# Sliding-window attention beside a gated MLP: exponentials of four steps in one buffer, far scores eight key blocks at a time

## The chip, the cores and the metric

The kernel runs on one core of a Trainium2 chip. The metric is the device time of one execution in microseconds, a median of several runs. The profile is one execution of its own, with every engine's instructions: TensorE (PE, and PEld for its weight loads), VectorE (DVE), ScalarE (ACT), GpSimd (POOL) and SyncE (SP), which only issues DMAs here.

## What is computed

The input has 2048 tokens of 512 features, in bf16. One branch is causal attention with 32 heads of 16 features and a window of 256 tokens, the other a gated MLP with 1376 hidden features. A sigmoid gate g per token mixes them.

```python
def _A_ref(x, wqkv, wo):
    H = 32; Dh = D // H; W = 256
    ...
    scores = jnp.einsum("bhqd,bhkd->bhqk", q, k) * (Dh ** -0.5)
    mask = (idx[:, None] - idx[None, :] >= 0) & (idx[:, None] - idx[None, :] < W)
    scores = jnp.where(mask[None, None], scores, -1e9)
    p = _softmax(scores, axis=-1)
    o = jnp.einsum("bhqk,bhkd->bhqd", p, v)
    return (o as B, S, D) @ wo

def _B_ref(x, w1, w3, w2):
    h = silu(x @ w1) * (x @ w3)
    return h @ w2

g = _sigmoid((x * gate_w).sum(-1, keepdims=True))
return g * a + (1 - g) * b
```

## The kernel before

**One order for all engines, made by a planner.** Nothing is issued where it stands in the source. Every piece of work is an `Op` with an engine, an assumed duration, its dependencies, a due time and the buffers it takes and frees. `Plan.emit` is a list scheduler: it steps through assumed time, and on the engine that can start first it picks, among the ops that can start within 0.02 us of that, the one with the earliest due time. The order that comes out is what each engine executes, first in, first out; the real waits are semaphores. The due times come from four constants: attention is spread from `T0` over `TA` microseconds (`at(c, t)`), the MLP from `TF0` to `TF1`.

**Attention.** The 32 heads are cut into four head groups c of eight heads (128 features), one after another, and the tokens into 16 steps t of 128. Scores are held transposed, keys in partitions and queries in columns. The keys of a step are two blocks of 64; a block of 64 keys of two heads fills 128 partitions (`kbd`, with zeros so that each head meets its own features), and four such pairs of heads run in the four 32-row groups of TensorE.

- `projections(c, tq)`: Q, K and V for a quarter of the tokens (tq = 0 to 3). K goes through VectorE (`kt`, L404) and two GpSimd multiplications (`kbd`, L407), for c = 0 through VectorE and ScalarE; Q is cast by VectorE (L418), V by ScalarE and VectorE (L437, L439).
- `main_batch(c, t)`: for both key blocks of a step, the scores against the block's own 64 queries and the 192 that follow, 8 matmuls of 256 columns (L464) into `su`, one buffer of four PSUM banks. Two exponentials on ScalarE (L469), two banks each, write columns 0 to 255 of an `E` buffer. VectorE masks the diagonal block with a minimum against `mdiag` (L476).
- `far_batch(c, g)`: the last, partly masked 64 queries of each key block (queries 256 to 319 after the block's start), for four key blocks at once: 16 matmuls of 64 columns (L499) into the same `su`, two exponentials (L504) into columns 256 to 319 of the two steps' `E` buffers, and two GpSimd affine selects for each (L512), one for each half of the partitions.
- `pv(c, i)`: for 128 queries, the products of up to six `E` slices with the values, 24 matmuls (L542) into a `ch` bank; the values carry a column of ones, so the softmax's sum comes along. VectorE takes the reciprocal (L550) and multiplies with it and with the gate (L553). SyncE transposes the result into `OT` by DMA (L559).

There are six `E` buffers, one taken by each step and freed by the pv two steps later.

**MLP and output.** For each quarter of the tokens, 11 blocks of hidden features: a gate chain (`gps`, one bank) and an up chain (`ups`, one bank) of four matmuls each (L603), a tanh on ScalarE (L608), and two VectorE products (L612 frees `gps`, L616 frees `ups`). Then w2 (L638), 11 matmuls for 128 tokens into a `ch` bank, scaled into `bsb` by VectorE (L642). The output projection (L662) needs `OT` of all four head groups; VectorE adds `bsb` (L666) and SyncE stores.

PSUM is full: `su` has four banks, `gps` and `ups` one each, and two `ch` banks serve projections, pv, w2 and output projection in turn. The score groups of all steps, main and far, go through the one `su`: a group's matmuls wait until the exponentials of the group before have read all of it.

Of the kernel before, what the change touches and what calls it, by code (L numbers as in the profile page):

```python
# [8 lines left out]
ACT = mybir.ActivationFunctionType  # L9
BF16 = mybir.dt.bfloat16  # L10
# [5 lines left out]
P = 128  # L16
KB = 64
# [20 lines left out]
class Plan:  # L38
# [73 lines left out]
def kernel(  # L112
# [12 lines left out]
    nc = tc.nc  # L125
# [13 lines left out]
    NE = 6  # L139
# [19 lines left out]
    kbd = pp.tile([P, NKB, 2, KB], BF16, name="kbd")  # L159
# [112 lines left out]
    def at(c, t):  # L272
        return T0 + step * (c * NT + t)
# [90 lines left out]
    ejob = {}  # L364

    def projections(c, tq):
# [52 lines left out]
        a = add("PE", 0.864, lambda: chain(qj, 0, 4), src + qwar, due, take=[(qj, "ch")])  # L419
        q_ready[(c, tq)] = add("DVE", 0.69, qev, [a], due, free=[(qj, "ch")])  # L420

        vj = Job()

# [24 lines left out]
            res.append(prev)  # L448
        v_ready[(c, tq)] = res

    def main_batch(c, t):
        due = at(c, t)
        job = Job()
        ej = ejob[(c, t)] = Job()
        wid = 256 if t < NT - 1 else P
        tqs = sorted({min(NTC - 1, (P * t) // 512), min(NTC - 1, (P * t + 319) // 512)})
        deps = list(k_ready[(c, t // 4)]) + [q_ready[(c, q)] for q in tqs]

        def mm():
            for par in range(2):  # L460
                q0 = KB * (2 * t + par)
                for s in range(4):
                    r = slice(32 * s, 32 * s + 32)
                    nc.tensor.matmul(su[:, s, par * wid:(par + 1) * wid],  # L464
                                     lhsT=kbd[r, 2 * t + par, :, :].rearrange("p a k -> p (a k)"),
                                     rhs=qT[r, q0:q0 + wid], start=True, stop=True)

        def ex(h):
            nc.scalar.activation(  # L469
                out=E[ej.at["E"]][:, 2 * h:2 * h + 2, :, 0:wid],  # L470
                in_=su[:, 2 * h:2 * h + 2, 0:2 * wid].rearrange("p s (a q) -> p s a q", a=2),
                func=ACT.Exp, scale=SCALE)

        def mask():
            e = E[ej.at["E"]][:, :, :, 0:KB].rearrange("p s a q -> p (s a) q")
            nc.vector.tensor_tensor(out=e, in0=e, in1=mdiag[:, None, :].to_broadcast([P, 8, KB]),  # L476
                                    op=ALU.min)
# [6 lines left out]
        return add("DVE", 0.42, mask, [x0, x1], due)  # L484

    def far_batch(c, g):
        t1 = 2 * g + 1
        due = at(c, t1) + 0.3
        job = Job()
        tq = min(NTC - 1, (P * (2 * g) + 511) // 512)  # L490
        deps = [q_ready[(c, min(NTC - 1, (KB * (4 * g + j) + 319) // 512))] for j in range(4)]
        deps += k_ready[(c, g // 2)]

        def mm():
            for j in range(4):
                q0 = KB * (4 * g + j) + 256
                for s in range(4):
                    r = slice(32 * s, 32 * s + 32)
                    nc.tensor.matmul(su[:, s, j * KB:(j + 1) * KB],  # L499
                                     lhsT=kbd[r, 4 * g + j, :, :].rearrange("p a k -> p (a k)"),  # L500
                                     rhs=qT[r, q0:q0 + KB], start=True, stop=True)

        def ex(i):
            nc.scalar.activation(  # L504
                out=E[ejob[(c, 2 * g + i)].at["E"]][:, :, :, 256:320],
                in_=su[:, :, i * P:(i + 1) * P].rearrange("p s (a q) -> p s a q", a=2),
                func=ACT.Exp, scale=SCALE)

        def mask(i):
            e = E[ejob[(c, 2 * g + i)].at["E"]][:, :, :, 256:320].rearrange("p s a q -> p (s a) q")  # L510
            for lo in (0, KB):
                nc.gpsimd.affine_select(out=e[lo:lo + KB], in_=e[lo:lo + KB], pattern=[[0, 8], [-1, KB]],  # L512
                                        compare_op=ALU.is_ge, fill=0.0, base=-1, channel_multiplier=1)

        a = add("PE", 0.4, mm, deps + [su_ops[(c, t1)]], due, take=[(job, "su")])
        far_ops[(c, g)] = a
        res = []
        for i in range(2):
            x = add("ACT", 0.54, lambda i=i: ex(i), [a], due, free=[(job, "su")])
            res.append(add("POOL", 1.28, lambda i=i: mask(i), [x], due))  # L520
        return res

    def pv(c, i, main, far):
        due = at(c, i) + 0.6
# [12 lines left out]
        def mm():  # L537
            po = ch[job.at["ch"]]
            for s in range(4):
                for bi, (t, par, off) in enumerate(blocks):  # L540
                    e = E[ejob[(c, t)].at["E"]][:, s].rearrange("p a q -> p (a q)")
                    nc.tensor.matmul(po[:, 34 * s:34 * s + 34], lhsT=e[:, off:off + P],  # L542
                                     rhs=vbd[:, 2 * t + par, s, :], start=(bi == 0),
                                     stop=(bi == len(blocks) - 1))
# [26 lines left out]
        ot_ready[(c, i)] = add("SP", 1.1, tr, [d], due, free=[(job, "oc")], lat=1.6)  # L571

    for c in range(NDC):
        main, far = {}, {}
        for tq in range(NTC):
            projections(c, tq)
        for t in range(NT):
            main[t] = main_batch(c, t)
            if t % 2 == 1 and t < NT - 2:
                far[t - 1], far[t] = far_batch(c, t // 2)  # L580
# [126 lines left out]
```

## Time and profile before

| what | value |
|---|---|
| runs before | 264.07, 263.88, 263.87 us; median 263.88 |
| the profiled execution | 264.46 us |
| its span, first to last instruction | 262.4 us |
| TensorE's granted clock | 1.000 |
| main score groups (L464) / far score groups (L499) / pv (L542) | 64 / 28 / 64 |
| main exponentials, 128 partitions x 1024 (L469) | 120, mean 1022 ns; 8 narrower ones of the last steps, 594 ns |
| far exponentials, 128 x 512 (L504) | 56, mean 595 ns |
| kbd multiplications on GpSimd, 128 x 512 (L407) | 24, mean 1605 ns |
| GpSimd affine select, 128 x 128 (ident, L191) | 1, 294 ns |
| TensorE idle before a score group, released by ScalarE (L464 and L499) | 1.4 us in all |

How to read it: the page gives for each engine its busy time as a share of the span, and then groups of instructions by line, engine and operation with count, total and mean duration, and the idle time of the engine just before them with what ended it. A matmul's end is modelled, and matmuls overlap, so durations of TensorE's groups do not add up; differences between starts do. In a list in order of time, the first number is the start in microseconds from the span's beginning and the second the length; a bracket at the end gives the engine's idle time before and what ended it. For TensorE's line numbers: L464 main scores, L499 far scores, L542 pv, L603 gate and up, L638 w2, L383 Q and K, L429 V, L662 output projection.

### The profile page before, as it was taken

How to read it: one execution, taken by the hardware profiler on the slowest of the kernel's cores; microseconds unless marked ns; L12 is line 12 of the kernel's file. 1: busy time of each engine (PE TensorE's matmuls, PEld its weight loads, DVE VectorE, ACT ScalarE, POOL GpSimd, SP SyncE). 2: the span in 40 equal slices, each digit the busy share in tenths (PEclk: the TensorE clock that was granted, in tenths of full speed). 3: DMA queues.
4: the chain of work that ended last, by engine and by line, in shares of the span. 5: the costliest groups of instructions: out<-in, count | busy, mean ns of one | idle time of the engine just before them, and what ended most of it. 6: DMA issues, size and time to landing. Idle time of an engine off the chain costs nothing.

```text
span 262.4 us, 8242 instructions
## 1 busy us (share of the span) xinstructions
PE 249.0 (95%) x3447; PEld 138.2 (53%) x3501; DVE 174.8 (67%) x393; ACT 190.3 (73%) x271; POOL 116.1 (44%) x157
## 2 busy tenths in 40 slices
PE   8999999999999999999999999999989999999992
PEld 8455564654555555555455445564546454455540
DVE  4576977845578867755487775766468867765652
ACT  3278798787677797777768888777677787776640
POOL 6003223662736635782273683751736233332220
PEclk9999999999999999999999999999999999999999
DMA  7999950000001000000000000000000111110112
GB/s 192 267 246 258 223 132 9 13 12 10 8 8 21 8 8 14 11 8 13 6 18 13 8 10 13 14 12 6 13 8 18 45 34 52 50 33 27 50 52 65
DMA packets 27933, 13.14 MB, mean 50 GB/s; under 512 B 17305, under 2 KB 27897, under 8 KB 27897
## 3 DMA queue, kind: packets, MB, share of 16 engines
q1 hardware_dynamic: 27896, 12.63, 21.6%
q8 instruction: 27, 0.44, 0.7%
q14 instruction: 10, 0.07, 0.1%
HBM read 6.85 MB, written 2.10 MB: 34 GB/s over the span
## 4 chain that ended last, share of the span: by engine, by line
PE 86%; ACT 3%; DVE 3%; DMA 2%; POOL 2%; issue 2%; SPq 0%
PE ch L638 14%; PE ch L542 14%; PE gps L603 14%; PE ups L603 13%; PE ch L383 10%; PE su L464 7%; PE ch L429 5%; PE ch L662 5%; DMA OT<-oc 2%; PE su L499 2%; ACT E L469 2%; POOL kbd L407 1%; PE su L225 1%; POOL E L512 1%; ACT vbd L437 1%
## 5 line engine op out<-in xcount | busy, mean ns | idle before, releaser
L469 ACT ACTIVATE E<-su 128x1024 bf16<-128x1024 f32 (+1 forms) x128 | 122.5, 995 | 28.0 <-PE su L464 27.6
L512 POOL TENSOR_SCALAR_AFFINE_SELECT E<-E 64x512 bf16<-64x512 bf16 x112 | 73.5, 656 | 107.3 <-ACT E L504 87.9
L542 PEld LDWEIGHTS <-E 128*128 128x128 bf16 x1440 | 43.3, 96 | 12.9 <-issue 4.6
L407 POOL TENSOR_SCALAR kbd<-kt,rowsA 128x512 bf16<-128x512 bf16 x24 | 38.3, 1605 | 26.5 <-DVE kt L404 11.9
L603 PEld LDWEIGHTS <-w_sb 128*128 128x128 bf16 (+1 forms) x352 | 31.3, 99 | 33.6 <-issue 4.8
L542 PE MATMUL ch<-vbd,E 128*128 128x34 bf16 x1440 | 46.4, 177 | 0.6 <-POOL E L512 0.4
L603 PE MATMUL gps<-xT,w_sb 128*128 128x512 bf16 (+1 forms) x163 | 43.5, 379 | 1.3 <-DVE h L612 0.5
L603 PE MATMUL ups<-xT,w_sb 128*128 128x512 bf16 (+1 forms) x156 | 43.0, 380 | 1.1 <-issue 0.2
L638 PE MATMUL ch<-w_sb,hT 128*128 128x512 bf16 (+1 forms) x161 | 42.6, 380 | 1.2 <-issue 0.5
L504 ACT ACTIVATE E<-su 128x512 bf16<-128x512 f32 x56 | 30.4, 595 | 13.4 <-PE su L499 12.1
L612 DVE SCALAR_TENSOR_TENSOR h<-tt,gps 128x512 bf16<-128x512 bf16 (+1 forms) x44 | 29.8, 678 | 14.8 <-ACT tt L608 14.1
L476 DVE TENSOR_TENSOR E<-E,mdiag 128x512 bf16<-128x512 bf16 x64 | 27.9, 437 | 16.1 <-ACT E L469 16.0
L608 ACT ACTIVATE tt<-gps 128x512 bf16<-128x512 f32 (+1 forms) x44 | 26.3, 598 | 13.5 <-PE gps L603 12.6
L616 DVE SCALAR_TENSOR_TENSOR hT<-h,ups 128x512 bf16<-128x512 bf16 (+1 forms) x44 | 29.9, 681 | 5.7 <-PE ups L603 4.4
L383 PE MATMUL ch<-xT,wqkv_sb 128*128 128x512 bf16 x126 | 32.5, 380 | 0.1
L464 PE MATMUL su<-qT,kbd 32*128 32x256 bf16 (+1 forms) x512 | 25.0, 269 | 1.6 <-ACT E L469 1.2
L550 DVE RECIPROCAL rden<-ch 128x8 f32<-128x8 f32 x64 | 13.1, 204 | 18.1 <-PE ch L542 17.8
L638 PEld LDWEIGHTS <-hT 128*128 128x128 bf16 (+1 forms) x176 | 14.9, 97 | 16.6 <-issue 2.9
L553 DVE SCALAR_TENSOR_TENSOR oc<-ch,gq,rden 128x128 bf16<-128x128 f32 x64 | 22.3, 349 | 1.5
L383 PEld LDWEIGHTS <-wqkv_sb 128*128 128x128 bf16 x128 | 11.5, 98 | 13.6 <-issue 1.4
L662 PE MATMUL ch<-wo_sb,OT 128*128 128x512 bf16 x60 | 16.1, 380 | 2.3 <-DMA OT<-oc 1.5
L464 PEld LDWEIGHTS <-kbd 32*128 32x128 bf16 x512 | 7.9, 92 | 19.3 <-issue 18.1
(55 smaller groups left out, 154.8 us busy)
## 6 DMA issues: line engine op xcount, KB each, us to landing
out_dram<-ot SPq DMA_DIRECT2D x16, 128.0 KB, 1.8
wqkv_sb<-in_A_wqkv_dram SPq DMA_DIRECT2D x6, 256.0 KB, 5.2
w_sb<-in_B_w_dram SPq DMA_DIRECT2D x1, 1280.0 KB, 7.1
w_sb<-in_B_w_dram SPq DMA_DIRECT2D x2, 608.0 KB, 5.3
w_sb<-in_B_w_dram SPq DMA_DIRECT2D x2, 512.0 KB, 6.8
OT<-oc SPq DMA_TRANSPOSE x64, 2.3
xs<-in_A_x_dram SPq DMA_DIRECT2D x2, 256.0 KB, 3.0
w_sb<-in_B_w_dram SPq DMA_DIRECT2D x2, 256.0 KB, 4.4
```

The source lines that it names most:

```text
L383: nc.tensor.matmul(pst[:], lhsT=wqkv_sb[:, dc, col + c * P:col + (c + 1) * P], rhs=xT[:, dc, tq * 512:(tq + 1) * 512], start=(dc == 0), st ...
L407: nc.gpsimd.tensor_scalar_mul(out=kv[:, :, h, :], in0=kt[kj.at["kt"]][:].rearrange("p (k t) -> p k t", t=KB), scalar1=rowsA[:, h:h + 1])
L464: nc.tensor.matmul(su[:, s, par * wid:(par + 1) * wid], lhsT=kbd[r, 2 * t + par, :, :].rearrange("p a k -> p (a k)"), rhs=qT[r, q0:q0 + wi ...
L469: nc.scalar.activation(out=E[ej.at["E"]][:, 2 * h:2 * h + 2, :, 0:wid], in_=su[:, 2 * h:2 * h + 2, 0:2 * wid].rearrange("p s (a q) -> p s ...
L504: nc.scalar.activation(out=E[ejob[(c, 2 * g + i)].at["E"]][:, :, :, 256:320], in_=su[:, :, i * P:(i + 1) * P].rearrange("p s (a q) -> p s ...
L512: nc.gpsimd.affine_select(out=e[lo:lo + KB], in_=e[lo:lo + KB], pattern=[[0, 8], [-1, KB]], compare_op=ALU.is_ge, fill=0.0, base=-1, chann ...
L542: nc.tensor.matmul(po[:, 34 * s:34 * s + 34], lhsT=e[:, off:off + P], rhs=vbd[:, 2 * t + par, s, :], start=(bi == 0), stop=(bi == len(bloc ...
L603: nc.tensor.matmul(dst[0:fs, :], lhsT=w[:, dc, f * P:f * P + fs], rhs=xT[:, dc, tcb * 512:(tcb + 1) * 512], start=(dc == 0), stop=(dc == N ...
L612: nc.vector.scalar_tensor_tensor(out=h1[job.at["h1"]][0:fs, :], in0=tt[job.at["tt"]][0:fs, :], scalar=1.0, in1=gps[0:fs, :], op0=ALU.add, ...
L616: nc.vector.scalar_tensor_tensor(out=hT[0:fs, f, :], in0=h1[job.at["h1"]][0:fs, :], scalar=0.5, in1=ups[0:fs, :], op0=ALU.mult, op1=ALU.mult)
L638: nc.tensor.matmul(bps[:], lhsT=hT[0:fs, f, mm * P:(mm + 1) * P], rhs=w2_sb[0:fs, f, :], start=(f == 0), stop=(f == NFC - 1))
L662: nc.tensor.matmul(pso[:], lhsT=OT[:, c, m * P:(m + 1) * P], rhs=wo_sb[:, c, :], start=(c == 0), stop=(c == NDC - 1))
```

## The change

`E` becomes two buffers, each for a quad of four steps (eight key blocks). A quad takes its buffer once, in an op without an instruction (`quad`, on an engine "EQ" that exists for the planner alone), and every pv frees the quads that it reads. A main step has one exponential over all four banks. The far scores of a quad's eight key blocks are one group: 32 matmuls that fill `su`, one exponential, and two affine selects over all eight blocks of the quad (the last quad of a head group has only four key blocks: 16 matmuls, half an exponential, and selects of the full size). The far batch no longer waits for a main batch of its own quad, and stands ahead of them in the list. Q of the later quarters gets an earlier due time, and the four constants of the due times change. In the order that the planner makes of it, each head group has 16 main and 4 far score groups, and a far group follows the first main group of its quad, for head group 0, quad 0 the second.

```diff
-    E = [pp.tile([P, 4, 2, 384], BF16, name=f"E_{i}") for i in range(NE)]
+    E = [pp.tile([P, 4, 8, 384], BF16, name=f"E_{i}") for i in range(2)]
...
-        for i in range(NE):
-            nc.gpsimd.memset(E[i][:, :, 0, 320:384], 0.0)
+        for e in E:
+            for s in range(4):
+                nc.gpsimd.memset(e[:, s, 0:8:2, 320:384], 0.0)
...
-    T0, TA, TF0, TF1 = 12.0, 218.0, 6.0, 252.0
+    T0, TA, TF0, TF1 = 9.0, 222.0, 6.0, 246.0
...
-            war += [far_ops.get((c - 1, g)) for g in (2 * tq, 2 * tq + 1)]
+            war.append(far_ops[(c - 1, tq)])
...
         qj = Job()
+        qdue = due if tq == 0 else at(c, 4 * tq - 4) - lead + 4.0
...
-    def main_batch(c, t):
+    def quad(c, h):
+
+        job = ejob[(c, h)] = Job()
+        return add("EQ", 0.0, lambda: None, [], at(c, 4 * h) - 1.0, take=[(job, "E")], lat=0.0)
+
+    def main_batch(c, t, room):
         due = at(c, t)
         job = Job()
-        ej = ejob[(c, t)] = Job()
+        ej = ejob[(c, t // 4)]
+        j0 = 2 * (t % 4)
...
-        def ex(h):
+        def ex():
             nc.scalar.activation(
-                out=E[ej.at["E"]][:, 2 * h:2 * h + 2, :, 0:wid],
-                in_=su[:, 2 * h:2 * h + 2, 0:2 * wid].rearrange("p s (a q) -> p s a q", a=2),
+                out=E[ej.at["E"]][:, :, j0:j0 + 2, 0:wid],
+                in_=su[:, :, 0:2 * wid].rearrange("p s (a q) -> p s a q", a=2),
                 func=ACT.Exp, scale=SCALE)
 
         def mask():
-            e = E[ej.at["E"]][:, :, :, 0:KB].rearrange("p s a q -> p (s a) q")
-            nc.vector.tensor_tensor(out=e, in0=e, in1=mdiag[:, None, :].to_broadcast([P, 8, KB]),
+            e = E[ej.at["E"]][:, :, j0:j0 + 2, 0:KB]
+            nc.vector.tensor_tensor(out=e, in0=e, in1=mdiag[:, None, None, :].to_broadcast([P, 4, 2, KB]),
                                     op=ALU.min)
...
-        x0 = add("ACT", d, lambda: ex(0), [a], due, take=[(ej, "E")], free=[(job, "su")])
-        x1 = add("ACT", d, lambda: ex(1), [a, x0], due, free=[(job, "su")])
+        x0 = add("ACT", 1.8 if wid == 256 else 1.0, ex, [a, room], due, free=[(job, "su")])
...
-    def far_batch(c, g):
-        t1 = 2 * g + 1
-        due = at(c, t1) + 0.3
+    def far_batch(c, h, room):
+
+        due = at(c, 4 * h) + 0.3
...
+        nb = min(8, NKB - 4 - 8 * h)
+        deps = [q_ready[(c, q)] for q in range(h, min(NTC, h + 2))] + k_ready[(c, h)]
 
         def mm():
-            for j in range(4):
-                q0 = KB * (4 * g + j) + 256
+            for j in range(nb):
+                q0 = KB * (8 * h + j) + 256
...
-        def ex(i):
+        def ex():
             nc.scalar.activation(
-                out=E[ejob[(c, 2 * g + i)].at["E"]][:, :, :, 256:320],
-                in_=su[:, :, i * P:(i + 1) * P].rearrange("p s (a q) -> p s a q", a=2),
+                out=E[ej.at["E"]][:, :, 0:nb, 256:320],
+                in_=su[:, :, 0:nb * KB].rearrange("p s (j q) -> p s j q", q=KB),
                 func=ACT.Exp, scale=SCALE)
 
-        def mask(i):
-            e = E[ejob[(c, 2 * g + i)].at["E"]][:, :, :, 256:320].rearrange("p s a q -> p (s a) q")
+        def mask():
+            e = E[ej.at["E"]][:, :, :, 256:320].rearrange("p s j q -> p (s j) q")
             for lo in (0, KB):
-                nc.gpsimd.affine_select(out=e[lo:lo + KB], in_=e[lo:lo + KB], pattern=[[0, 8], [-1, KB]],
+                nc.gpsimd.affine_select(out=e[lo:lo + KB], in_=e[lo:lo + KB],
+                                        pattern=[[0, 32], [-1, KB]],
                                         compare_op=ALU.is_ge, fill=0.0, base=-1, channel_multiplier=1)
 
-        a = add("PE", 0.4, mm, deps + [su_ops[(c, t1)]], due, take=[(job, "su")])
-        far_ops[(c, g)] = a
-        res = []
-        for i in range(2):
-            x = add("ACT", 0.54, lambda i=i: ex(i), [a], due, free=[(job, "su")])
-            res.append(add("POOL", 1.28, lambda i=i: mask(i), [x], due))
-        return res
+        a = add("PE", 0.52 if nb == 8 else 0.4, mm, deps, due, take=[(job, "su")])
+        far_ops[(c, h)] = a
+        x = add("ACT", 1.8 if nb == 8 else 1.0, ex, [a, room], due, free=[(job, "su")])
+        return [add("POOL", 5.2, mask, [x], due)] * (nb // 2)
...
-        frees = []
-        if i >= 2:
-            frees.append((ejob[(c, i - 2)], "E"))
-        if i == NT - 1:
-            frees += [(ejob[(c, i - 1)], "E"), (ejob[(c, i)], "E")]
+        frees = [(ejob[(c, h)], "E") for h in range(max(0, i - 2) // 4, i // 4 + 1)]
```

More of the change, by code (lines that the diff above doesn't have):

```diff
@@ L138 @@
     SCALE = float(DH) ** -0.5
-    NE = 6
     WARM = 28
@@ L182 @@
     ch = [ps.tile([P, 512], F32, name=f"ch_{i}") for i in range(2)]
-    plan = Plan({"su": 1, "g": 1, "u": 1, "ch": 2, "E": NE, "kt": 2, "tt": 2, "h1": 2,
+    plan = Plan({"su": 1, "g": 1, "u": 1, "ch": 2, "E": 2, "kt": 2, "tt": 2, "h1": 2,
                  "oc": 8, "ot": 2, "hT": 1})
@@ L371, in projections @@
             war = [su_ops[(c - 1, t)] for t in range(4 * tq, 4 * tq + 4)]
-            war += [far_ops.get((c - 1, g)) for g in (2 * tq, 2 * tq + 1)]
+            war.append(far_ops[(c - 1, tq)])
             vwar = [pv_ops[(c - 1, i)] for i in range(4 * tq, min(NT, 4 * tq + 6))]
             qwar = [su_ops[(c - 1, t)] for t in range(max(0, 4 * tq - 3), 4 * tq + 4)]
-            qwar += [far_ops.get((c - 1, g)) for g in range(max(0, 2 * tq - 2), 2 * tq + 2)]
+            qwar += [far_ops[(c - 1, h)] for h in range(max(0, tq - 1), tq + 1)]
         else:
@@ L415, in projections @@
         qj = Job()
+        qdue = due if tq == 0 else at(c, 4 * tq - 4) - lead + 4.0
         def qev():
             nc.vector.tensor_copy(out=qT[:, tq * 512:(tq + 1) * 512], in_=ch[qj.at["ch"]][:])
-        a = add("PE", 0.864, lambda: chain(qj, 0, 4), src + qwar, due, take=[(qj, "ch")])
-        q_ready[(c, tq)] = add("DVE", 0.69, qev, [a], due, free=[(qj, "ch")])
+        a = add("PE", 0.864, lambda: chain(qj, 0, 4), src + qwar, qdue, take=[(qj, "ch")])
+        q_ready[(c, tq)] = add("DVE", 0.69, qev, [a], qdue, free=[(qj, "ch")])
         vj = Job()
@@ L466, in mm @@
                                      rhs=qT[r, q0:q0 + wid], start=True, stop=True)
-        def ex(h):
+        def ex():
             nc.scalar.activation(
-                out=E[ej.at["E"]][:, 2 * h:2 * h + 2, :, 0:wid],
-                in_=su[:, 2 * h:2 * h + 2, 0:2 * wid].rearrange("p s (a q) -> p s a q", a=2),
+                out=E[ej.at["E"]][:, :, j0:j0 + 2, 0:wid],
+                in_=su[:, :, 0:2 * wid].rearrange("p s (a q) -> p s a q", a=2),
                 func=ACT.Exp, scale=SCALE)
         def mask():
-            e = E[ej.at["E"]][:, :, :, 0:KB].rearrange("p s a q -> p (s a) q")
-            nc.vector.tensor_tensor(out=e, in0=e, in1=mdiag[:, None, :].to_broadcast([P, 8, KB]),
+            e = E[ej.at["E"]][:, :, j0:j0 + 2, 0:KB]
+            nc.vector.tensor_tensor(out=e, in0=e, in1=mdiag[:, None, None, :].to_broadcast([P, 4, 2, KB]),
                                     op=ALU.min)
         a = add("PE", 0.42 if wid == 256 else 0.31, mm, deps, due, take=[(job, "su")])
-        d = 0.833e-3 * 4 * wid + 0.1
-        x0 = add("ACT", d, lambda: ex(0), [a], due, take=[(ej, "E")], free=[(job, "su")])
-        x1 = add("ACT", d, lambda: ex(1), [a, x0], due, free=[(job, "su")])
+        x0 = add("ACT", 1.8 if wid == 256 else 1.0, ex, [a, room], due, free=[(job, "su")])
         su_ops[(c, t)] = a
-        return add("DVE", 0.42, mask, [x0, x1], due)
-    def far_batch(c, g):
-        t1 = 2 * g + 1
-        due = at(c, t1) + 0.3
+        return add("DVE", 0.42, mask, [x0], due)
+    def far_batch(c, h, room):
+        due = at(c, 4 * h) + 0.3
         job = Job()
-        tq = min(NTC - 1, (P * (2 * g) + 511) // 512)
-        deps = [q_ready[(c, min(NTC - 1, (KB * (4 * g + j) + 319) // 512))] for j in range(4)]
-        deps += k_ready[(c, g // 2)]
+        ej = ejob[(c, h)]
+        nb = min(8, NKB - 4 - 8 * h)
+        deps = [q_ready[(c, q)] for q in range(h, min(NTC, h + 2))] + k_ready[(c, h)]
         def mm():
-            for j in range(4):
-                q0 = KB * (4 * g + j) + 256
+            for j in range(nb):
+                q0 = KB * (8 * h + j) + 256
                 for s in range(4):
@@ L499, in mm @@
                     nc.tensor.matmul(su[:, s, j * KB:(j + 1) * KB],
-                                     lhsT=kbd[r, 4 * g + j, :, :].rearrange("p a k -> p (a k)"),
+                                     lhsT=kbd[r, 8 * h + j, :, :].rearrange("p a k -> p (a k)"),
                                      rhs=qT[r, q0:q0 + KB], start=True, stop=True)
-        def ex(i):
+        def ex():
             nc.scalar.activation(
-                out=E[ejob[(c, 2 * g + i)].at["E"]][:, :, :, 256:320],
-                in_=su[:, :, i * P:(i + 1) * P].rearrange("p s (a q) -> p s a q", a=2),
+                out=E[ej.at["E"]][:, :, 0:nb, 256:320],
+                in_=su[:, :, 0:nb * KB].rearrange("p s (j q) -> p s j q", q=KB),
                 func=ACT.Exp, scale=SCALE)
-        def mask(i):
-            e = E[ejob[(c, 2 * g + i)].at["E"]][:, :, :, 256:320].rearrange("p s a q -> p (s a) q")
+        def mask():
+            e = E[ej.at["E"]][:, :, :, 256:320].rearrange("p s j q -> p (s j) q")
             for lo in (0, KB):
-                nc.gpsimd.affine_select(out=e[lo:lo + KB], in_=e[lo:lo + KB], pattern=[[0, 8], [-1, KB]],
+                nc.gpsimd.affine_select(out=e[lo:lo + KB], in_=e[lo:lo + KB],
+                                        pattern=[[0, 32], [-1, KB]],
                                         compare_op=ALU.is_ge, fill=0.0, base=-1, channel_multiplier=1)
-        a = add("PE", 0.4, mm, deps + [su_ops[(c, t1)]], due, take=[(job, "su")])
-        far_ops[(c, g)] = a
-        res = []
-        for i in range(2):
-            x = add("ACT", 0.54, lambda i=i: ex(i), [a], due, free=[(job, "su")])
-            res.append(add("POOL", 1.28, lambda i=i: mask(i), [x], due))
-        return res
+        a = add("PE", 0.52 if nb == 8 else 0.4, mm, deps, due, take=[(job, "su")])
+        far_ops[(c, h)] = a
+        x = add("ACT", 1.8 if nb == 8 else 1.0, ex, [a, room], due, free=[(job, "su")])
+        return [add("POOL", 5.2, mask, [x], due)] * (nb // 2)
     def pv(c, i, main, far):
@@ L540, in mm @@
                 for bi, (t, par, off) in enumerate(blocks):
-                    e = E[ejob[(c, t)].at["E"]][:, s].rearrange("p a q -> p (a q)")
+                    e = E[ejob[(c, t // 4)].at["E"]][:, s, 2 * (t % 4):2 * (t % 4) + 2, :].rearrange("p a q -> p (a q)")
                     nc.tensor.matmul(po[:, 34 * s:34 * s + 34], lhsT=e[:, off:off + P],
@@ L573 @@
     for c in range(NDC):
-        main, far = {}, {}
+        main = {}
         for tq in range(NTC):
             projections(c, tq)
[L577 to L580, printed above, removed]
+        far = []
+        for h in range(NTC):
+            room = quad(c, h)
+            far += far_batch(c, h, room)
+            for t in range(4 * h, 4 * h + 4):
+                main[t] = main_batch(c, t, room)
         for i in range(NT):
```

## The prediction

> **What bounds the kernel now.** I read the page's busy line first, then TensorE's instructions in order of time, then the waits, then VectorE and GpSimd around the masks.
>
> ```profile
> span 262.4 us, 8242 instructions
> PE 249.0 (95%) x3447; PEld 138.2 (53%) x3501; DVE 174.8 (67%) x393; ACT 190.3 (73%) x271; POOL 116.1 (44%) x157
> ...
> L469 ACT ACTIVATE E<-su 128x1024 bf16<-128x1024 f32 (+1 forms) x128 | 122.5, 995 | 28.0 <-PE su L464 27.6
> L512 POOL TENSOR_SCALAR_AFFINE_SELECT E<-E 64x512 bf16<-64x512 bf16 x112 | 73.5, 656 | 107.3 <-ACT E L504 87.9
> ...
> L476 DVE TENSOR_TENSOR E<-E,mdiag 128x512 bf16<-128x512 bf16 x64 | 27.9, 437 | 16.1 <-ACT E L469 16.0
> ```
>
> TensorE is busy in 95% of the span and every other engine has idle time. ScalarE's exponentials wait for TensorE (27.6 us before L469), not the other way. So shortening ScalarE pays only where TensorE waits for it.
>
> ```profile
> 228.30 1.03 PE L603 MATMUL gps<-xT,w_sb 128*96 128x512 bf16 x4
> 229.26 0.40 PE L464 MATMUL su<-qT,kbd 32*128 32x256 bf16 x8
> 229.59 0.77 PE L542 MATMUL ch<-vbd,E 128*128 128x34 bf16 x24
> 230.21 1.02 PE L662 MATMUL ch<-wo_sb,OT 128*128 128x512 bf16 x4
> 231.06 1.03 PE L603 MATMUL ups<-xT,w_sb 128*96 128x512 bf16 x4
> 232.02 0.30 PE L499 MATMUL su<-qT,kbd 32*128 32x64 bf16 x16
> 232.25 0.77 PE L542 MATMUL ch<-vbd,E 128*128 128x34 bf16 x24
> ```
>
> Columns: start, length, work. Read starts to starts, since lengths overlap. Four matmuls of 512 columns take 0.86 us (230.21 to 231.06), but 0.96 if a score group follows (228.30 to 229.26): 0.10 to enter a score group. A main group takes 0.33, a far group of 16 takes 0.23, a pv of 24 takes 0.62 (0.69 before a score group), a v projection 0.89.
>
> I priced the whole issue order with these steps: 250.05 us. TensorE's first matmul starts at 1.04 and its last ends near 258.55, so it waits 258.55 - 1.04 - 250.05 = 7.5 us. Comparing the starts of all 92 score groups with the priced order places them: 0.8 us before 15 us, 4.6 between 15 and 245, 2.1 at the end. After the last matmul come 3.85 us of evacuation and store. That is the check on my ruler: 250.05 + 1.04 + 0.8 + 4.6 + 2.1 + 3.85 = 262.4.
>
> **The change, part by part.**
>
> *Far scores in batches of eight.* The changed order has 16 far groups (12 of 32 matmuls, 4 of 16) for 28. A group of 32 moves as many columns as a main group of 8x256, so I take 0.34; two old groups, 0.46, are the other bound (12 x 0.12 = 1.4 us more). Far matmuls go from 28 x 0.23 = 6.44 to 12 x 0.34 + 4 x 0.23 = 5.0, and 12 entries of 0.10 vanish. The same pricing over the changed order gives 247.5 us: 2.6 off TensorE's own path.
>
> *One exponential for four banks.* One of 1024 elements takes 1.022 us, one of 512 takes 0.594: 0.836 ns an element and 0.166 fixed, so 2048 take 1.88. The old pair overlaps itself and takes 1.94 (two at 186.64 end at 188.58). The score banks are thus held 0.06 us less; the main group before a far group holds them for as long as before, and a wide far exponential holds them 1.88 for 1.08. Start to start a score group now needs 0.33 + 0.12 (to ScalarE) + 1.88 + 0.06 (back) = 2.39. Along the new order all but five gaps give that; those lack 0.48, 0.30, 0.21, 0.08 and 0.07. The 0.30 comes ahead of a wait counted below, so 0.8. Where a pv follows its own main mask too early, six places lack 1.3 together. So 2.1 new against the 4.6 of old waits in the middle, which were made by another order; some of those go. I take 5.5 for both, bounds 3.5 and 6.7.
>
> *Shared E buffers.* A quad needs the buffer of two quads earlier. Its first writer starts 2.5 us or more of TensorE work after the last pv that read it, in every quad. Nothing.
>
> *Moved Q projections, and the new due times.* They show only in the order. The clearest part is the end.
>
> ```profile
> 254.45 0.76 PE L542 MATMUL ch<-vbd,E 128*128 128x34 bf16 x24
> 255.39 0.81 PE L662 MATMUL ch<-wo_sb,OT 128*128 128x512 bf16 x2 [0.18 <-DVE ot L666]
> 256.48 1.04 PE L662 MATMUL ch<-wo_sb,OT 128*128 128x512 bf16 x4 [0.28 <-DMA OT<-oc]
> 258.34 0.39 PE L662 MATMUL ch<-wo_sb,OT 128*128 128x512 bf16 x1 [0.82 <-DMA OT<-oc]
> ```
>
> Now the last output projections wait for the transposing DMA of the last pv. In the changed order 22 w2 matmuls (4.7 us) and a projection lie between the last pv and the last two projections, longer than reciprocal, product and DMA (about 3 us). I leave 0.3 of the 2.1.
>
> *The far mask, which speaks against the change.* It is one affine select on 64x2048 for four on 64x512. From 128x128 (0.294) to 512 elements (0.657) it costs 0.945 ns an element, so 2.11 us; bounds 2.1 and 4 x 0.657 = 2.63. GpSimd's total falls (32 x 2.11 = 67.5 for 73.5), but one instruction is three times as long. What that does to VectorE:
>
> ```profile
> 169.22 0.66 POOL L512 TENSOR_SCALAR_AFFINE_SELECT E<-E 64x512 bf16<-64x512 bf16 x1
> ...
> 169.28 0.87 DVE L476 TENSOR_TENSOR E<-E,mdiag 128x512 bf16<-128x512 bf16 x1 [0.33 <-ACT E L469]
> ...
> 186.58 3.13 POOL L407 TENSOR_SCALAR kbd<-kt,rowsA 128x512 bf16<-128x512 bf16 x2 [0.90 <-DVE kt L404]
> ...
> 188.76 0.41 DVE L476 TENSOR_TENSOR E<-E,mdiag 128x512 bf16<-128x512 bf16 x1
> ```
>
> The main mask L476, usually 0.42, took 0.87 when it began 0.06 us into an affine select, and ended 0.27 after that one's end. Another, at 146.29, took 0.80 and ended 0.28 after its affine select. A third, at 154.09, began 0.15 before an end and lost nothing. So the mask stands still until the running select is over. Only three of 64 masks met one. Under kbd (L407) it does not stand still: 12 of 16 overlaps cost nothing, the worst 0.18.
>
> The Trainium skill, "SBUF — State Buffer", section "Who interferes with whom", says that a VectorE instruction with two SBUF inputs and a GpSimd instruction that reads SBUF exclude each other for the whole instruction. The select rows agree with it; the kbd rows do not. By the rule the sum is the likeliest case below, by the kbd rows the first rival.
>
> In the new order the meeting is built in. Count from the end of a far group of 32. Its exponential ends at 0.12 + 1.88 = 2.00; the two selects run 2.08 to 6.36. The next main group starts at about 2.44, its exponential runs from 2.9 to 4.8, its mask would start at 4.85, inside the second select, and ends at 6.63 in place of 5.27: 1.36 late. The pv that reads it can start at 6.70. Behind a far group of 16 (exponential 1.02) the bound is 5.88. When does TensorE reach that pv? For head group 1, quad 1: pv 0.62 + gate 0.86 + projection 0.96 + main 0.33 + up 0.86 + gate 0.86 + v 0.89 = 5.38, so it waits 1.3. All 16 in turn (0 where it comes later): 0, 0.50, 0, 0.31; 0.65, 1.32, 0.92, 0.07; 1.51, 1.35, 0.27, 1.17; 2.00, 0.92, 0.05, 1.17. Sum 12.2 us. Behind the late mask VectorE has the up and gate products, the Q and K casts and the pv quotients queued; TensorE's wait of about the same length gives them their time back, except where the wait is short, and there they may add some. Bounds of this part: 3.1 if a mask never loses more than the 0.45 seen (the pv can then start at 5.80, or 4.94 behind a far group of 16), and 16 x 1.36 = 21.8 if VectorE's whole delay reaches TensorE. I take 12.2, by the three rows that end with the select.
>
> In this case a pv that waits lets the others' producers catch up, so of the 5.5 I keep 3.5.
>
> *Sum*, against the profiled span: 247.5 + 1.04 + 0.8 + 3.5 + 12.2 + 0.3 + 3.85 = 269.2, that is 6.8 more than 262.4. The profiled run took 264.46 in all, the median of the runs is 263.88; on that, 270.7 us. The two other edits, mask constants at the start and the wider mask operand on VectorE (again 512 elements), cost nothing: the constants run while TensorE waits for loads, and 0.1 us more on a mask would be 0.1 per short pv, 1.2 at most.
>
> **Rivals.**
>
> *The mask slips past long selects* (as under kbd). Then the 12.2 is gone and 5.5 stays: 259.0 span, 260.5 us, faster. For it: GpSimd has room and 12 of 16 kbd overlaps are free. Against it: every mask that met a select early in it stood still. It decides for gain once the mean loss at a pv falls below 0.2 us.
>
> *The mask loses at most 0.45.* Then 3.1 + 5.5: 262.1 span, 263.6 us, level with before. For it: no longer loss has been seen; against it: none could be, with selects of 0.66.
>
> *VectorE's delay spreads.* If each 1.36 reaches TensorE also through the gate bank (freed by L612) and the two ch banks, 21.8 for 12.2: 280.3 us. For it: gate and up have one bank each. Against it: VectorE is 67% busy and catches up.
>
> **How the numbers follow.** Likeliest case 0.62, slips past 0.23, at most 0.45 lost 0.12, spreads 0.03. Its own range is 267 to 274 (3.5 to 6.7 of other waits, far groups at 0.46). The range for 8 in 10 has to reach into the first rival: 260.0 to 274.0. A measurement here tells about 0.2%, 0.5 us, from no change. Faster: 0.23 of the first rival and half of the second's 0.12, less a little for the bound: 0.29. Same 0.06. Slower: 0.62 and 0.03: 0.65.
>
> **What would show it.** Right: affine selects near 2.1 us; some 14 to 16 main masks of 1 to 2.2 us, each ending 0.27 after a select; TensorE idle before pv with VectorE's mask or GpSimd as releaser, about 10 to 14 us; no wait on the DMA in the last projections; 80 score groups, a far group of 32 starting its successor 0.34 later. Wrong: masks all near 0.42, or selects well under 1.6 us (the second would end before the mask), and then a time near 260.5.

## The result, and the profile after

The changed kernel takes 276.16 us (275.92 to 276.2) against 263.88: a ratio of 1.0462, interval 1.0444 to 1.0481. It is slower, as forecast, but by 12.3 us instead of 6.8, and the time lies 2.2 us above the range.

The page of the changed kernel, its span, busy times and three groups:

```profile
span 274.1 us, 8026 instructions
...
PE 248.6 (91%) x3450; PEld 137.3 (50%) x3501; DVE 198.2 (72%) x393; ACT 183.0 (67%) x167; POOL 110.4 (40%) x79
...
L517 POOL TENSOR_SCALAR_AFFINE_SELECT E<-E 64x2048 bf16<-64x2048 bf16 x32 | 67.8, 2120 | 119.1 <-ACT E L509 118.1
L483 DVE TENSOR_TENSOR E<-E,mdiag 128x512 bf16<-128x512 bf16 x64 | 48.4, 756 | 16.7 <-ACT E L476 16.7
L545 PE MATMUL ch<-vbd,E 128*128 128x34 bf16 x1440 | 48.1, 178 | 11.6 <-DVE E L483 8.4
```

ScalarE and GpSimd became less busy, VectorE 23 us busier, although it has the same 393 instructions. Most of that is in one line: the 64 main masks, 27.9 us before, take 48.4 us. At 0.415 us for an undisturbed one, 21.8 us of it is standing still.

The waits of TensorE after (engine, line, what it waited for; us in all, times, longest), from 0.5 us on, without the start and its own issue:

```profile
PE ch L545 <- DVE E L483: 8.4, 9, 1.5
PE gps L604 <- DVE h L613: 2.0, 3, 1.1
...
PE ch L383 <- DVE vbd L440: 1.0, 1, 1.0
PE ch L639 <- DVE vbd L440: 1.0, 1, 1.0
PE ch L545 <- DVE bsb L643: 1.0, 2, 0.8
...
PE ch L545 <- DVE vbd L440: 0.8, 1, 0.8
...
PE ch L545 <- DVE kt L404: 0.7, 1, 0.7
...
PE ch L545 <- DVE ot L667: 0.5, 1, 0.5
```

The first line is the forecast mechanism, pv waiting for the mask it reads. The others shown add up to 7.0 us, and none of them names the mask: a gate bank or a `ch` bank was not emptied in time by VectorE. Some 2 us of the 7.0 do not come from the change of the selects; e2 below has them too.

One of the stuck masks, in head group 3 (start, length, work, idle time before; instructions of several engines):

```profile
205.63 4.28 POOL L517 TENSOR_SCALAR_AFFINE_SELECT E<-E 64x2048 bf16<-64x2048 bf16 x2 [9.90 <-ACT E L509]
206.06 1.88 ACT L476 ACTIVATE E<-su 128x2048 bf16<-128x2048 f32 x1 [0.50 <-PE su L471]
...
207.97 2.21 DVE L483 TENSOR_TENSOR E<-E,mdiag 128x512 bf16<-128x512 bf16 x1 [0.19 <-ACT E L476]
...
210.24 0.52 PE L545 MATMUL ch<-vbd,E 128*128 128x34 bf16 x14 [1.45 <-DVE E L483]
```

The second select ends at 205.63 + 4.28 = 209.91, the mask at 210.18: 0.27 later. In 15 of 16 quads there is such a mask, and all 15 end 0.26 to 0.28 after a select. They stand still for 20.4 us together, 1.36 on the mean; most of the rest of the 21.8 is three other masks that met a kbd multiplication (last section).

### The profile page after: what moved, and what is told of

The parts are those of the page before. It is cut to its first block, busy times and chain, and to the rows that moved or that the text cites. A ratio compares the mean times of both kernels' runs of the same rounds, so it can differ in the third digit from the quotient of the medians.

```text
span 274.1 us, 8026 instructions
## 1 busy us (share of the span) xinstructions
PE 248.6 (91%) x3450; PEld 137.3 (50%) x3501; DVE 198.2 (72%) x393; ACT 183.0 (67%) x167; POOL 110.4 (40%) x79
## 4 chain that ended last, share of the span: by engine, by line
PE 69%; DVE 15%; ACT 9%; issue 5%; another core or an unknown queue 0%; ACTq 0%
PE ch L545 13%; PE ups L604 11%; PE gps L604 10%; PE ch L639 10%; PE ch L383 8%; DVE E L483 7%; ACT E L476 6%; PE su L471 6%; PE ch L663 5%; PE ch L430 3%; DVE vbd L440 2%; PE su L504 2%; DVE bsb L643 1%; ACT vbd L438 1%; PE su L225 1%
## 5 line engine op out<-in xcount | busy, mean ns | idle before, releaser
L476 ACT ACTIVATE E<-su 128x2048 bf16<-128x2048 f32 x64 | 116.6, 1822 | 44.3 <-PE su L471 44.0
L517 POOL TENSOR_SCALAR_AFFINE_SELECT E<-E 64x2048 bf16<-64x2048 bf16 x32 | 67.8, 2120 | 119.1 <-ACT E L509 118.1
L483 DVE TENSOR_TENSOR E<-E,mdiag 128x512 bf16<-128x512 bf16 x64 | 48.4, 756 | 16.7 <-ACT E L476 16.7
L545 PE MATMUL ch<-vbd,E 128*128 128x34 bf16 x1440 | 48.1, 178 | 11.6 <-DVE E L483 8.4
L407 POOL TENSOR_SCALAR kbd<-kt,rowsA 128x512 bf16<-128x512 bf16 x24 | 37.6, 1579 | 26.4 <-DVE kt L404 23.2
L639 PE MATMUL ch<-w_sb,hT 128*128 128x512 bf16 (+1 forms) x165 | 42.0, 379 | 2.1 <-DVE vbd L440 1.0
L613 DVE SCALAR_TENSOR_TENSOR h<-tt,gps 128x512 bf16<-128x512 bf16 (+1 forms) x44 | 30.0, 681 | 10.8 <-ACT tt L609 10.0
L383 PE MATMUL ch<-xT,wqkv_sb 128*128 128x512 bf16 x122 | 31.9, 379 | 1.5 <-DVE vbd L440 1.0
L509 ACT ACTIVATE E<-su 128x2048 bf16<-128x2048 f32 (+1 forms) x16 | 26.6, 1662 | 8.4 <-PE su L504 8.4
L553 DVE RECIPROCAL rden<-ch 128x8 f32<-128x8 f32 x64 | 13.1, 204 | 12.7 <-PE ch L545 12.2
L643 DVE TENSOR_SCALAR bsb<-ch,omg 128x512 bf16<-128x512 f32 x16 | 11.8, 747 | 8.3 <-PE ch L639 8.2
```

Source lines behind the costliest of these rows:

```text
L407: nc.gpsimd.tensor_scalar_mul(out=kv[:, :, h, :], in0=kt[kj.at["kt"]][:].rearrange("p (k t) -> p k t", t=KB), scalar1=rowsA[:, h:h + 1])
L476: nc.scalar.activation(out=E[ej.at["E"]][:, :, j0:j0 + 2, 0:wid], in_=su[:, :, 0:2 * wid].rearrange("p s (a q) -> p s a q", a=2), func=ACT ...
L483: nc.vector.tensor_tensor(out=e, in0=e, in1=mdiag[:, None, None, :].to_broadcast([P, 4, 2, KB]), op=ALU.min)
L509: nc.scalar.activation(out=E[ej.at["E"]][:, :, 0:nb, 256:320], in_=su[:, :, 0:nb * KB].rearrange("p s (j q) -> p s j q", q=KB), func=ACT.E ...
L613: nc.vector.scalar_tensor_tensor(out=h1[job.at["h1"]][0:fs, :], in0=tt[job.at["tt"]][0:fs, :], scalar=1.0, in1=gps[0:fs, :], op0=ALU.add, ...
L639: nc.tensor.matmul(bps[:], lhsT=hT[0:fs, f, mm * P:(mm + 1) * P], rhs=w2_sb[0:fs, f, :], start=(f == 0), stop=(f == NFC - 1))
```

## The experiments

Each run's middle waits are TensorE's waits from its first score group to its last, read as in the prediction: starts of the score groups against the issue order at undisturbed prices. Mask delay is the busy time of VectorE's main masks beyond 0.415 us each.

| kernel | median us | ratio to before (interval) | mask delay | middle waits |
|---|---|---|---|---|
| before | 263.88 | | 1.4 | 4.6 |
| changed | 276.16 | 1.0462 (1.0444 to 1.0481) | 21.8 | 21.1 |
| e1, selects cut in four | 261.12 | 0.9884 (0.9869 to 0.9900) | 4.0 | 6.2 |
| e2, memset for select | 260.93 | 0.9870 (0.9851 to 0.9890) | 1.6 | 5.3 |
| e3, far mask on VectorE | 265.32 | 1.0037 (1.0024 to 1.0051) | 1.9 | 9.4 |
| e4, before plus long selects | 280.73 | 1.0630 (1.061 to 1.065) | 26.8 | 19.3 |
| e5, latency told | 273.31 | 1.0346 (1.0301 to 1.0391) | 19.5 | 15.6 |
| e6, busy time told | 271.37 | 1.0286 (1.0260 to 1.0312) | 16.1 | 15.0 |
| e7, cut, old T0 and TA | 266.87 | 1.0105 (1.0060 to 1.0151) | 4.2 | 10.7 |
| e8, cut, exponential halved | 261.64 | 0.9913 (0.9894 to 0.9932) | 3.7 | 6.4 |
| e9, stuck mask on GpSimd | 261.20 | 0.9882 (0.9853 to 0.9911) | 2.4 | 5.6 |
| e10, cut, latency told | 264.08 | 1.0007 (0.9991 to 1.0022) | 3.8 | 6.1 |
| e11, cut, mask on GpSimd | 263.70 | 0.9975 (0.9961 to 0.9988) | 1.4 | 7.7 |

### e1: the far selects cut in four

```diff
-            e = E[ej.at["E"]][:, :, :, 256:320].rearrange("p s j q -> p (s j) q")
-            for lo in (0, KB):
-                nc.gpsimd.affine_select(out=e[lo:lo + KB], in_=e[lo:lo + KB],
-                                        pattern=[[0, 32], [-1, KB]],
+            for s in range(4):
+                e = E[ej.at["E"]][:, s, :, 256:320]
+                for lo in (0, KB):
+                    nc.gpsimd.affine_select(out=e[lo:lo + KB], in_=e[lo:lo + KB],
+                                            pattern=[[0, 8], [-1, KB]],
```

> The changed kernel with each far select cut into four of 64x512; order of all other work unchanged. Theory A (a main mask stands still until the running select ends, and VectorE's queue behind it hands the delay to TensorE): a mask can lose at most about 0.5 us instead of 2.1, so the 21.8 us of mask delay fall to about 5, and the time to 264 to 267 us. Theory B (the new order and due times cost the time, whatever the selects do): 276 us, unchanged.

261.12 us, 15 us less with TensorE's order unchanged, and faster than before. The page of this run:

```profile
L518 POOL TENSOR_SCALAR_AFFINE_SELECT E<-E 64x512 bf16<-64x512 bf16 x128 | 86.2, 673 | 103.7 <-ACT E L509 97.2
L483 DVE TENSOR_TENSOR E<-E,mdiag 128x512 bf16<-128x512 bf16 x64 | 30.6, 478 | 17.6 <-ACT E L476 17.5
```

GpSimd works 18 us more than in the changed kernel (86.2 for 67.8), and the kernel is 15 us faster: the length of one select decided, not their sum. Theory B (order and due times) falls. The time lies under the 264 to 267 of Theory A: masks still lose 4.0 us, 1.9 of them under the short selects and nearly all the rest under kbd multiplications, but that hardly reaches TensorE (middle waits 6.2 against 5.3 in e2).

### e2: memsets in the selects' place

```diff
-                nc.gpsimd.affine_select(out=e[lo:lo + KB], in_=e[lo:lo + KB],
-                                        pattern=[[0, 32], [-1, KB]],
-                                        compare_op=ALU.is_ge, fill=0.0, base=-1, channel_multiplier=1)
+                nc.gpsimd.memset(e[lo:lo + KB], 0.0)
```

> The changed kernel with the far selects replaced by GpSimd memsets of the same elements, which write and do not read (the far scores are left out of the sums). Order and dependencies unchanged, GpSimd busy nearly as long. Theory A: main masks back to 0.42 us each, TensorE's waits in the middle down from 21 to about 5 us, 260 to 262 us. Theory B: 276 us. If GpSimd being late with the far mask were the cause: also 275 us or so, since the memsets are about as long (1.7 for 2.1 us).

260.93 us. The page of this run, and two lines of its waits of TensorE:

```profile
L517 POOL MEMSET E<- 64x2048 bf16 x32 | 57.5, 1798 | 115.8 <-ACT E L509 115.0
L483 DVE TENSOR_TENSOR E<-E,mdiag 128x512 bf16<-128x512 bf16 x64 | 28.2, 441 | 18.1 <-ACT E L476 18.0
...
PE gps L602 <- DVE h L611: 1.0, 2, 0.5
PE ch L637 <- DVE vbd L440: 1.0, 1, 1.0
```

The memsets take 1.80 us each, close to the select's 2.12, with the same dependencies, and no mask stands still because of them. So it is not that GpSimd is late or that VectorE meets any GpSimd work: it is the long select itself. That it is the select's read of SBUF is not shown by this run alone, since a memset differs from a select in more than that. It agrees with the section of the Trainium skill that the prediction cites ("SBUF — State Buffer", "Who interferes with whom"), which makes the same difference between GpSimd instructions that read and those that only write.

Since the order is the same, this run prices the stuck masks quad by quad: the time from one far group to the next, changed kernel minus e2.

| quad (head group, quad) | forecast wait at pv, us | measured, us |
|---|---|---|
| 0,0 / 0,1 / 0,2 / 0,3 | 0 / 0.50 / 0 / 0.31 | 1.18 / 0.57 / 1.21 / 0.96 |
| 1,0 / 1,1 / 1,2 / 1,3 | 0.65 / 1.32 / 0.92 / 0.07 | 0.66 / 1.31 / 1.16 / 0.91 |
| 2,0 / 2,1 / 2,2 / 2,3 | 1.51 / 1.35 / 0.27 / 1.17 | 0 / 1.33 / 0.90 / 1.09 |
| 3,0 / 3,1 / 3,2 / 3,3 | 2.00 / 0.92 / 0.05 / 1.17 | 1.62 / 1.26 / 0.69 / 1.02 |
| sum | 12.2 | 15.9 |

The table falls into three parts. In the nine quads with a forecast wait of 0.50 or more and a stuck mask, 10.0 us were forecast and 10.0 measured (single quads are off by up to 0.4). There TensorE's wait is at pv, on the mask: the nine waits of 8.4 us above; from start to start each costs some 0.17 us more than its idle time. The six quads with 0.31 or less were forecast at 0.70 together and cost 5.85. There TensorE's wait names another VectorE instruction each time, one that empties a bank: at 28.86, 58.66, 72.27, 135.62, 182.80 and 242.69, 4.9 us in all, none of which e2 has. In 2,0 no mask got stuck: two kbd multiplications stood ahead of the selects, which began at 146.52, and the mask at 148.61 fell between the two. The 1.51 forecast there did not come, which the prediction had not seen.

Quad 0,2 of the changed kernel, one of the six, shows where the cost comes from when pv does not wait:

```profile
52.87 4.29 POOL L517 TENSOR_SCALAR_AFFINE_SELECT E<-E 64x2048 bf16<-64x2048 bf16 x2 [3.97 <-ACT E L509]
...
55.65 1.78 DVE L483 TENSOR_TENSOR E<-E,mdiag 128x512 bf16<-128x512 bf16 x1 [1.29 <-ACT E L476]
...
56.06 0.60 ACT L609 ACTIVATE tt<-gps 128x512 bf16<-128x512 f32 x1
...
57.46 0.43 DVE L440 CAST vbd<-ch 64x256 bf16<-64x256 f32 x1
57.92 0.69 DVE L613 SCALAR_TENSOR_TENSOR h<-tt,gps 128x512 bf16<-128x512 bf16 x1
...
58.66 1.02 PE L604 MATMUL gps<-xT,w_sb 128*128 128x512 bf16 x4 [1.05 <-DVE h L613]
```

and the same work in e2, some 1.5 us earlier in its span:

```profile
54.16 0.43 DVE L483 TENSOR_TENSOR E<-E,mdiag 128x512 bf16<-128x512 bf16 x1 [1.29 <-ACT E L476]
54.57 0.60 ACT L607 ACTIVATE tt<-gps 128x512 bf16<-128x512 f32 x1
54.61 0.43 DVE L440 CAST vbd<-ch 64x256 bf16<-64x256 f32 x1
...
55.20 0.69 DVE L611 SCALAR_TENSOR_TENSOR h<-tt,gps 128x512 bf16<-128x512 bf16 x1 [0.15 <-ACT tt L607]
...
55.96 1.03 PE L602 MATMUL gps<-xT,w_sb 128*128 128x512 bf16 x4
```

The gate product (L613, here L611) starts 2.27 us after the mask's start with the long select, and 1.04 us without. It empties the one gate bank; TensorE's next gate chain stands there and waits 1.05 us. The pv of this mask comes later still and never waits for it.

### e3: the far mask on VectorE

```diff
-                nc.gpsimd.affine_select(out=e[lo:lo + KB], in_=e[lo:lo + KB],
...
+            e = E[ej.at["E"]][:, :, 0:nb, 256:320]
+            nc.vector.tensor_tensor(out=e, in0=e, in1=fdiag[:, None, None, :].to_broadcast([P, 4, nb, KB]),
+                                    op=ALU.min)
```

> The changed kernel with the far mask as one VectorE minimum over 128x2048 in place of two GpSimd selects, at the same place of the order. Theory A: no mask is held up, VectorE gets 16 x about 1.2 = 19 us more work, which it has room for in part: 260 to 264 us. Theory B: 276 us or more, since VectorE only gets more work.

265.32 us: over the expected 264, though no select is left and masks lose only 1.9 us. The new instruction:

```profile
L522 DVE TENSOR_TENSOR E<-E,fdiag 128x2048 bf16<-128x2048 bf16 x12 | 14.7, 1223 | 3.7 <-ACT E L515 3.5
```

With its four short ones that is 17.4 us of work, for 19 expected; middle waits are 4.1 us longer than in e2. So a long instruction in VectorE's queue cost TensorE time here without any select: about a quarter of what it lasts got through.

### e4: the cause added to the kernel before

```diff
+        def extra():
+            for lo in (0, KB):
+                nc.gpsimd.affine_select(out=scr[lo:lo + KB], in_=scr[lo:lo + KB], pattern=[[0, 32], [-1, KB]],
+                                        compare_op=ALU.is_ge, fill=0.0, base=-1, channel_multiplier=1)
+        if g % 2 == 1 or g == 6:
+            add("POOL", 0.0, extra, [res[1]], due)
```

> The kernel before, with 16 pairs of extra GpSimd selects of 64x2048 on a scratch buffer that nobody reads, one pair after every second far batch; order of all else unchanged. Theory A: the extra selects hold main masks for up to 2.1 us each, some 15 to 25 us of mask delay, of which more than half reaches TensorE: 272 to 282 us. Theory B: nothing depends on them, 264 us (up to 266 if GpSimd's kbd comes late).

280.73 us, 16.5 us more than the kernel before beside it (264.27), by instructions whose result nobody reads.

```profile
L526 POOL TENSOR_SCALAR_AFFINE_SELECT scr<-scr 64x2048 bf16<-64x2048 bf16 x32 | 68.8, 2151 | 1.8
L478 DVE TENSOR_TENSOR E<-E,mdiag 128x512 bf16<-128x512 bf16 x64 | 53.3, 833 | 14.5 <-ACT E L471 14.5
```

The masks lose 26.8 us, 25.4 more than before. This also occupies GpSimd for longer, but far masks or kbd that come late behind the extra selects do not account for it: TensorE waits for GpSimd 0.4 us and VectorE's `kt` 2.5, once each, and both waits stand in the kernel before as well.

### e5, e6 and e9: pv's own wait, or the queue behind the mask

All three keep the long selects. e5 and e6 change what the planner reckons for the stuck mask, e9 moves this mask.

```diff
e5
-        return add("DVE", 0.42, mask, [x0], due)
+        return add("DVE", 0.42, mask, [x0], due, lat=1.5 if t % 4 == 1 else 0.08)
e6
+        return add("DVE", 1.9 if t % 4 == 1 else 0.42, mask, [x0], due)
e9
+        if t % 4 == 1:
+            def gmask():
+                for j in (j0, j0 + 1):
+                    e = E[ej.at["E"]][:, :, j, 0:KB]
+                    for lo in (0, KB):
+                        nc.gpsimd.affine_select(out=e[lo:lo + KB], in_=e[lo:lo + KB], pattern=[[0, 4], [1, KB]],
+                                                compare_op=ALU.is_ge, fill=0.0, base=0, channel_multiplier=-1)
+            return add("POOL", 1.7, gmask, [x0], due)
```

> The changed kernel with its long selects, but the planner reckons 1.5 us of latency behind the main mask of the first step after each far batch (the op occupies VectorE 0.42 us as before), so that TensorE reaches the pv that reads it later. Theory A1 (the loss is TensorE waiting at that pv, and nearly nothing else): the waits on the mask, 8 us or more, vanish, and with them most of the loss: 262 to 265 us. Theory A2 (VectorE's queue behind the stuck mask costs as well, through the gate bank and the two ch banks): masks still lose some 20 us, the waits on the mask vanish, the others stay or grow: 267 to 273 us.

273.31 us, 0.3 above the range of Theory A2. The waits of TensorE in e5:

```profile
PE gps L604 <- DVE h L613: 3.1, 6, 0.8
PE ch L383 <- DVE vbd L440: 2.5, 1, 2.5
...
PE ch L639 <- DVE vbd L440: 1.0, 1, 1.0
PE ch L639 <- DVE hT L617: 0.8, 1, 0.8
...
PE ch L545 <- DVE E L483: 0.2, 1, 0.2
```

The 8.4 us at the mask are down to 0.2, masks still lose 19.5, and the time falls by less than 3 us: the wait moved to the banks that VectorE empties. The granted clock was 0.989 to 0.996 in these executions, 1.000 in the changed kernel's profile. By an estimate that lets the whole span go with the clock, the profiled span of 269.5 would be about 1.1 us shorter at 1.000, and the fall about 6 us; the time would still be 270 to 271, far above the 262 to 265 of Theory A1, which falls.

> The same, but the planner reckons that this mask occupies VectorE for 1.9 us, so it also plans for what is queued behind it. Theory A2: VectorE still loses some 20 us, but the waits on its casts and products shrink too: 262 to 267 us, clearly under the run with latency alone. Theory A1: the same as with latency alone.

271.37 us: 2 us under e5, the right way, but above 262 to 267. With clocks of 0.985 to 0.994, some 1.5 to 4 us of it is the clock by the same estimate, which leaves 268 to 269. Masks still lose 16.1 us, and a planner that knows of it covers only a part.

> The changed kernel with its long selects, but the main mask that gets stuck (first step after a far batch, t mod 4 = 1) is made by GpSimd itself behind the far selects, four selects of 64x256, and the planner knows it (1.7 us on GpSimd), so the pv comes later as in the run with told latency. VectorE has no stuck mask there. Theory A2 (the queue behind the stuck VectorE mask is what remained in that run): mask delay on VectorE falls from 20 to under 5 us, 261 to 265 us, against 273 with latency alone. Theory A1 (only the pv's own wait counts, the rest of that run came from its changed order): 270 us or more, as there.

261.20 us, 12 us under e5, with the same long selects. Part of that is the clock: the profiled executions, 261.69 us at 0.999 and 271.21 at 0.996, are 9.5 us apart.

```profile
L525 POOL TENSOR_SCALAR_AFFINE_SELECT E<-E 64x2048 bf16<-64x2048 bf16 x32 | 67.7, 2114 | 82.1 <-ACT E L517 81.2
L494 POOL TENSOR_SCALAR_AFFINE_SELECT E<-E 64x256 bf16<-64x256 bf16 x64 | 27.3, 427 | 18.5 <-ACT E L476 14.9
L483 DVE TENSOR_TENSOR E<-E,mdiag 128x512 bf16<-128x512 bf16 x48 | 22.3, 465 | 15.7 <-ACT E L476 15.2
```

Of the other 48 masks one stands still for 1.7 us (head group 0, where the first far group follows the second main group); the rest lose 0.7 together. pv is planned late in both e5 and e9; what e9 takes away is the standstill of VectorE's queue. It also takes 16 masks, 6.6 us of work, off VectorE; by the quarter of e3 that is worth under 2 us. The orders of e5 and e9 differ, so the 9.5 us are no exact price.

### e7, e8, e10, e11: what else is in the changed kernel, and the best version

e7 is e1 with `T0, TA, TF0, TF1 = 12.0, 218.0, 6.0, 246.0`; e8 is e1 with the main exponential in a loop over two halves of the banks, `for s in (0, 2)`; e10 is e1 with `lat=0.6 if t % 4 == 1 else 0.08` for the main mask; e11 is e1 with e9's `gmask`.

> The changed kernel with selects cut into 64x512 and the attention's due times of before (T0 12, TA 218; TF1 stays 246, since with 252 the planner finds no free buffer). If the due times carry part of the gain: 262 to 264 us, against 261.1 with the new ones. If not: 261 within 0.5.

266.87 us, outside both expectations, but the granted clock was 0.987 in most of its executions, which alone, by the same estimate, is about 3.4 us of a span of 264.7. What is left, some 2 us over e1, is no clean price for the due times. This stays open.

> The changed kernel with selects cut into 64x512 and each main exponential in two halves again (same order). The halves take 1.94 us together for 1.88, so the score banks are held 0.06 us longer in 60 steps. If those banks set TensorE's pace: up to 3.6 us more, 264 us. If TensorE sets its own pace: within 0.5 of 261.1 us.

261.64 us, 0.5 more than e1, at the edge of what the second case allows; the profiled spans are 259.7 and 259.8. TensorE sets its own pace, and the single exponential as such is worth next to nothing.

> The changed kernel with selects of 64x512, and 0.6 us of latency told to the planner for the first mask after a far batch. If the 4 us of mask delay left in the split kernel still cost TensorE: 259.5 to 260.5 us. If they are already covered: 261 or, by a less lucky order, more.

264.08 us. The mask delay stayed (3.8), the middle waits too (6.1), and the new order ends badly: two pv after the last score group wait 1.0 us for a `ch` bank, and the last matmuls are 11 of w2, after the last output projection, so a scaling, an addition and a store follow them (4.6 us from the last matmul's end in the profile, 3.4 in the changed kernel).

> Selects of 64x512 and the first main mask after a far batch on GpSimd (four selects of 64x256). Under theory A2 as the run with long selects and that mask on GpSimd, or up to 2 us less, since other masks that meet a select lose 0.5 instead of 2.1: 260 to 263 us.

263.70 us, above the expectation and above e1 and e9. TensorE now waits for GpSimd: 1.9 us in five pv, since selects of 64x512 take 83.8 us in all where the long ones took 67.7, and the masks stand behind them. Of the kernels that leave nothing out, e1 and e9 are the fastest, 1.2% under before and not told apart.

## Why the prediction was off

- **TensorE's own path, 2.6 us less: nothing speaks against it.** The order priced at 247.5, the start and the waits found add up to TensorE's last end at 270.5, but the middle waits are what the priced order leaves over, so this is no test of 247.5 by itself. What can be read alone agrees: in quad 0,2 the far group of 32 starts its successor 0.34 us later (50.37 to 50.71).
- **Durations: right.** Exponential 1.88 forecast, 1.875 measured; select 2.11 forecast, 2.12 measured.
- **The lock: right.** The 15 stuck masks end 0.26 to 0.28 after a select and stand still for 1.36 us on the mean, as forecast; e1, e2 and e4 shorten, replace and add the cause.
- **No gain from the held banks: right** (e8). **The end: nearly right**, 0.7 us of waits for 0.3, none on the DMA of the last projections.
- **The price of the stuck mask, 12.2 us: wrong, 15.9.** The failed step is the one that put VectorE's queue behind the mask at nothing: "TensorE's wait of about the same length gives them their time back, except where the wait is short, and there they may add some". The exception was named and not priced. Six quads with short waits cost 5.2 us more than forecast, as e2 shows, each at a bank that VectorE emptied late; e5, whose pv hardly waits for the mask and which has an order of its own, keeps 10.3 of the 15.8 us of middle waits that stuck masks add (15.6 and 21.1 against 5.3; about 1 of the 10.3 is the clock). The price of pv's own wait held: 10.0 for 10.0 in nine quads. In 2,0 no mask got stuck, and the 1.5 us saved there hid part of the error: that was luck. So the sign that the prediction named, 10 to 14 us of idle time before pv on the mask, came as 8.4.
- **"Of the 5.5 I keep 3.5": wrong.** The 5.5 itself was nearly right: e2, with the same order and no stuck masks, waits 5.3 us in the middle. That a waiting pv would take 2 us off them did not come: every middle wait over 0.12 us in the trace of e2 (0.5, 0.3, 0.2, 1.0, 0.2, 0.3, 0.2 and 0.1) stands in the changed kernel too, in the same place and of the same length.

The two make 3.7 + 1.8 = 5.5 us; the span is 4.9 us longer than forecast, since the wait before the first score group (0.16 for 0.8) and the last evacuation and store (3.6 for 3.85) gave back more than the end took. The range ended at 274.0 because it added 3.2 us to 270.7, the other waits at 6.7 for 3.5; the 1.4 us of its own bound for the far groups would already have made it 275.3, and the price of the stuck mask had no room in it. The rival in which all of the delay reaches TensorE, at a chance of 0.03, was too dear: 15.9 of 20.2 us (the measured 21.8 less e2's 1.6) did, about 0.8. The rival without a lock was priced at 260.5, and e2 measured 260.93.

## What to carry to other kernels

A GpSimd affine select held a VectorE instruction with two SBUF inputs until it ended, at 0.66 us as at 2.12; so the length of a single instruction counts, and making one of four can lose more than it saves. When a VectorE instruction stands still, price what is queued behind it as well as its reader: each PSUM bank that VectorE empties is a second place where TensorE stops, and here it counted most where the reader itself was well covered. When a merge changes several things, cutting one instruction back to its old length and leaving the order alone is a cheap and sharp test.

## What was not expected of the hardware

The kbd multiplication on GpSimd (L407, 1.58 us for 512 elements) also holds the mask, but only in its first part. In the changed kernel:

```profile
45.80 3.11 POOL L407 TENSOR_SCALAR kbd<-kt,rowsA 128x512 bf16<-128x512 bf16 x2 [3.72 <-DVE kt L404]
...
47.42 0.88 DVE L483 TENSOR_TENSOR E<-E,mdiag 128x512 bf16<-128x512 bf16 x1
```

The second multiplication starts at 47.34; the mask that begins 0.08 later ends at 48.30, and if it needs the same 0.27 after its release, it was released 0.69 into a multiplication of 1.56. In the kernel before, the changed one and e2, nine masks begin early in a multiplication and lose time, and all nine end 0.60 before its end. The mask at 188.76 in the kernel before, 0.6 into one, lost nothing. That fits a hold of about 0.7 us in which the data are read, but that it is the reading was not tried by itself.

The granted clock fell below 1.000 in some executions, most of all in one batch (0.985 to 0.996 in e5, e6 and e7, while e8 beside them had 1.000). In the profiles of e6 and e7 it is one short stretch: one slice of 40 at 0.5 in e6, two at 0.7 in e7. Why is open.
